# Retention and a routed MoE on one core: scores in 64x64 products without the empty corner, and each state update one step earlier

## The chip, the cores and the metric

The kernel runs on one core of a Trainium2 chip. The metric is the time of one execution on the device in microseconds (us); the kernel before has a median of 399.66 us over three runs. The engines are TensorE (PE; PEld are its weight loads), VectorE (DVE), ScalarE (ACT), GpSimd (POOL) and the transfer queues (SP issues most transfers). Each engine works through its own list in order.

## The reference

q, k and v have 4 batches, 8 heads, 768 positions and 64 dimensions per head. Each head carries a 64x64 state along the positions, and the result then goes, token by token, through one of 8 experts:

```python
for t in range(S):
    state = gamma * state + outer(k[:, :, t], v[:, :, t])      # gamma: one number per head
    y[:, :, t] = scale * q[:, :, t] @ state
x = y.transpose(0, 2, 1, 3).reshape(3072, 512)
expert = argmax(x @ w_gate, axis=1); p = softmax(x @ w_gate)
out[t] = p[t, expert] * (relu(x[t] @ w1[expert]) @ w2[expert])    # 512 -> 1024 -> 512
```

## The kernel before, in words

**Retention.** The 3072 positions are 24 chunks (`g`) of 128, six to a batch (`c = g % 6`). The heads are 4 pairs: `p` counts pairs, `r` is the half of the 128 partitions that a head of the pair sits on, and `p = 2 * m + o`. For each chunk:

- `load` (L217) brings q and k (turned, dimension on the partitions) and v and k (natural, position on the partitions), 1 MB. Chunks 0 to 4 come in two halves, later ones in one transfer. `scale` (L232) multiplies v by powers of gamma and gives `vs`, on GpSimd or, where the caller says so, on VectorE.
- `scores` (L242) makes k times q per head: 8 products of 64 rows by 128 columns, 128 columns moving, into two PSUM tiles `sp`, one for each `r`. Of each 128x128 result the part where a key lies behind its query is not wanted: VectorE multiplies each tile by the mask `causal` (L251) and gives `Sb`.
- `carry` (L268) multiplies the state after the chunk before (`ub`) by q into the PSUM tile `Y`; the first chunk of a batch has none. `output` (L280) adds `Sb` times `vs` to `Y`; VectorE multiplies `Y` by decay factors `G` into `xT` (L293), which frees `Y`.
- `update` (L255) adds k times `vs` to the state `U` in PSUM, and ScalarE copies it to `ub` (L266). The last chunk of a batch has none.
- `rows` (L297) turns `xT` back into token rows with transposes, and `logits` (L328) and `finish_logits` (L338) make the gate's logits for two chunks at a time.

**Gate.** The chunks are in groups (`GROUPS`, L44). For each group `choose` (seven VectorE instructions, L371 to L380, of which L378 writes `EA`) picks the expert of each token, `rank` (TensorE, L385) counts places, `slots`, `weights`, `advance` (VectorE) finish them, and GpSimd's `send_rows` (L314) scatters the rows of the tokens into one region per expert. Group 2 are chunks 12 to 15, group 3 chunks 16 and 17.

**Order.** The schedule is written by hand: the loop at L530 calls these steps in the order in which each engine gets them. In pass `g` TensorE has scores of chunk `g + 1`, carry of `g`, then on even passes the transposes, on some the logits or a ranking, then the update of `g` and the output of `g`. Ahead of the loop (L472 to L512) stand the first loads, ten matmuls on `ones` that keep TensorE busy (`warm`, L489), the masks, scores of chunk 0 and the matmul `decay`. After the loop the last groups are ranked, with pieces of the first expert's work (`early_pieces`, L780) set between as `fill`; these need the rows of 320 tokens, which `turn_early` (L439) turns and splits.

**Experts.** `moe_main` (L826) runs the experts 1 to 7, each in a dense stream of matmuls with two-part weights (`split`, L127). `put_rows` (L870) weighs and scatters the last rows of the last expert.

Of the kernel before, what the change touches and what calls it, by code (L numbers as in the profile page):

```python
# [20 lines left out]
P = 128  # L21
NP = H // 2
C = 128
CPB = S // C
# [17 lines left out]
WARM = 10  # L42
# [12 lines left out]
for _name, _w in (("cv", 6 * H), ("ratio", 6 * (H // 2)), ("iota", E), ("desc", E), ("tok4", NTOK), ("blk", NJ), ("ebase", E),  # L55
                  ("rev", E1), ("eid", E1), ("caps", E1), ("quad", 1), ("slot", 16), ("pos", 4), ("gates", NP * E),
                  ("ahead", P), ("causal", P), ("ident", P)):
    OFF[_name] = (_n, _n + _w)
    _n += _w
NCONST = _n  # L60
NFIRST = OFF["iota"][0]
NLOAD = OFF["ahead"][0]


def _constants():
    p = np.arange(P)
    c = np.zeros((P, NLOAD), np.float64)

    def put(name, v):
        a, b = OFF[name]  # L70
        c[:, a:b] = v

    gamma = 1.0 - 2.0 ** (-5.0 - np.arange(H, dtype=np.float64))
    put("iota", np.broadcast_to(p[None, 0:E].astype(np.float64), (P, E)))
    pos = (np.arange(6)[None, :] * C + p[:, None] + 1).astype(np.float64)
    put("cv", (gamma[None, None, :] ** (-pos[:, :, None])).reshape(P, 6 * H))
# [18 lines left out]
def retention_moe(ctx, tc, qkv, w1, w2, cst, gdec, out):  # L95
# [8 lines left out]
    causal = k_("causal")  # L104
# [93 lines left out]
    with ExitStack() as actx:  # L198
# [5 lines left out]
        ps_s = apool("ps_s", 2, space=PS)  # L204
# [19 lines left out]
        def turned(g, i):  # L224
            return qs[g][:, i].rearrange("a (p t) -> a p t", p=NP)
# [15 lines left out]

        def scores(g):  # L242
            Sb = wk.tile([P, 2, NP, C], F32, name="Sb")
            q, kt = turned(g, 0), turned(g, 1)
            sps = [ps_s.tile([P, NP, C], F32, name="sp") for _ in range(2)]
            for p in range(NP):
                for r in range(2):
                    nc.tensor.matmul(out=sps[r][:, p, :], lhsT=kt[half[r], p, :], rhs=q[half[r], p, :],  # L248
                                     start=True, stop=True)
            for r in range(2):  # L250
                nc.vector.tensor_tensor(out=Sb[:, r], in0=sps[r],  # L251
                                        in1=causal.unsqueeze(1).broadcast_to([P, NP, C]), op=ALU.mult)
            Sbs[g] = Sb
# [14 lines left out]
        def carry(g):  # L268
            c = g % CPB
            Y = Ys[g] = ps_1.tile([P, 2, DM], F32, name="Y", tag="Y")  # L270
            if c > 0:
                q = turned(g, 0)
                for m in range(2):
                    for o in range(2):
                        p = 2 * m + o
                        for r in range(2):
                            nc.tensor.matmul(out=Y[half[o], r, m * C:(m + 1) * C], lhsT=ubs[(g - 1) % 3][half[r], p, :],
                                             rhs=q[half[r], p, :], start=(m == 0), stop=False, skip_group_check=True)
# [18 lines left out]
        def rows(g, ps=None, tag="mm"):  # L297
# [4 lines left out]
            tr = (ps or ps_m).tile([P, NP, P], F32, name="tr", tag=tag)  # L302
# [25 lines left out]
        def logits(t):  # L328
            pool_, tag = (ps_m, "mt") if t in slow else (ps_s, "sp") if 2 * t + 2 >= NCH - 2 else (ps_1, "misc")
            L = pool_.tile([P, TW], F32, name="L", tag=tag)  # L330
# [108 lines left out]
        def turn_early(i):  # L439
# [3 lines left out]
            if i == 0:  # L443
                first["xt"] = rawp.tile([P, KD, EARLY], F32, name="xt0", tag="raw")
                first["x"] = [wp.tile([P, KD, EARLY], F32R, name=n, tag="w", bufs=11) for n in ("xh0", "xl0")]
                early.extend(early_pieces(tc, wk, wp, ps_m, ps_s, ps_1, wparts, first["x"], first))
            xt0, x = first["xt"], first["x"]
            part = pieces[1:] if i else pieces[:1]
            for j, w, _ in part:
                turn_slices(nc, xt0, first["xg"], j, w)  # L450
            for j, w, _ in part:
                cut_high(nc, x[0], xt0, j, w)
            for j, w, eng in part:
# [39 lines left out]
        ahead = k_("ahead")  # L493
        nc.gpsimd.iota(ahead, pattern=[[1, P]], base=0, channel_multiplier=-1, allow_small_or_imprecise_dtypes=True)
        for mask, test in ((causal, ALU.is_ge), (ident, ALU.is_equal), (us, ALU.is_gt)):
            nc.vector.tensor_scalar(out=mask, in0=ahead, scalar1=0.0, scalar2=None, op0=test)
        nc.vector.memset(run, 0.0)
# [8 lines left out]
        scale(0, nc.vector)  # L506
# [22 lines left out]
        last = NCH - 1  # L529
        for g in range(NCH):  # L530
# [10 lines left out]
            if g in ranked:  # L541
# [16 lines left out]
            if g == FULL + 1:  # L558
                update(g)
# [12 lines left out]
            if c < CPB - 1 and g not in (1, FULL + 1):  # L572
# [21 lines left out]
            if g in chosen or g == last:  # L594
                i = chosen.get(g, 4)
                s = stages[i] = gating(i)
                s["choose"]()
                s["soft"]()
            if g == last:
                mark_early()  # L600
            if g in ranked:
# [3 lines left out]
                if g != FULL + 1:  # L605
                    s["slots"]()
                s["advance"]()
# [25 lines left out]
        rows(last, ps_s, "sp")  # L633
# [146 lines left out]
def early_pieces(tc, wk, wp, ps_m, ps_s, ps_1, wparts, x, first):  # L780
# [22 lines left out]
    def result(f, part):  # L803
        if not accs:
            accs.extend(ps_s.tile([P, DM], F32, name="acc", tag="sp") for _ in range(2))
# [20 lines left out]
def moe_main(ctx, tc, wparts, fetch, split, xhl1, Z0, ident, buf, xg, fetch_rows, expert_at, mask7, slot_marks, natural, overflow,  # L826
# [43 lines left out]
    def put_rows(e, py, j):  # L870
# [3 lines left out]

        parts = (slice(0, 2), slice(2, 4)) if e == E1 and j == len(widths[e]) - 1 else (slice(0, 4),)
        for i, k in enumerate(parts):
            args = dict(out=sliced(yo[:w, :])[:, k], in_=featured(py[:w, :])[:, k])
            if i:
                nc.scalar.activation(func=AF.Copy, scale=meta[:w, j, 1:2], **args)
            else:  # L880
                nc.vector.tensor_scalar(in0=args["in_"], out=args["out"], scalar1=meta[:w, j, 1:2], scalar2=None,
                                        op0=ALU.mult)
# [290 lines left out]
```

## Time and profile before

| | |
|---|---|
| median of 3 runs | 399.66 us (399.08 to 399.91) |
| the profiled execution | 400.06 us |
| its span, first to last instruction | 398.3 us |
| TensorE busy | 390.3 us (98%), 3236 matmuls and 3236 weight loads |
| VectorE, ScalarE, GpSimd busy | 240.3, 142.4, 185.2 us |
| moved by transfers | 81.53 MB, mean 205 GB/s |

The profile is of one execution, so sums are made against its own time and then set against the median. A busy time is that in which at least one instruction of the engine is under way; matmuls overlap, so their starts say more than their busy time. An idle time stands with the engine that waited and with what released it; "issue" means that the profile shows no releaser.

### The profile page before, as it was taken

To read this page: it belongs to the slowest core of one execution; us is meant where nothing else is said; L and a number is where in the kernel's file an instruction comes from. 1 tells how busy PE (TensorE), PEld (TensorE's weight loads), DVE (VectorE), ACT (ScalarE), POOL (GpSimd) and SP (SyncE) were. 2 spreads that over 40 slices of the span, in tenths; PEclk is the share of its full clock that TensorE was granted. 3 is DMA by queue.
4 is the path that set the end of the run, shared out by engine and by line. 5 is a ranking of instruction groups with operands and counts; after the bars stand their busy time and mean duration, and the time that the engine had idled before them with its cause. 6 is when DMAs were issued, how large, how long until landed. Compare 5 with 4: busy or idle time off the path is not lost. (4 is left out here: it accounts for less than half of the span.)

```text
span 398.3 us, 8240 instructions
## 1 busy us (share of the span) xinstructions
PE 390.3 (98%) x3236; PEld 356.5 (89%) x3236; DVE 240.3 (60%) x468; ACT 142.4 (36%) x249; POOL 185.2 (46%) x176
## 2 busy tenths in 40 slices
PE   8999999999999999999999999999999999999994
PEld 4888878787899889999999999999999999999972
DVE  3555757685744578573866477477737657665310
ACT  2224435224411455531542344054334416423100
POOL 1647959655260517200584077028406813740741
PEclk9999999999999999999999999999999999999998
DMA  8999999975058839547452755465564647430111
GB/s 273 422 419 420 418 416 420 324 297 149 2 216 174 327 117 305 214 167 162 166 182 92 190 183 213 84 209 165 177 152 157 234 83 232 146 133 0 54 47 48
DMA packets 42316, 81.53 MB, mean 205 GB/s; under 512 B 4444, under 2 KB 18144, under 8 KB 39844
## 3 DMA queue, kind: packets, MB, share of 16 engines
q1 hardware_dynamic: 36768, 67.46, 51.2%
q0 software_dynamic: 5360, 13.49, 9.1%
q8 instruction: 26, 0.43, 0.4%
q14 instruction: 14, 0.11, 0.1%
q10 hardware_dynamic: 148, 0.04, 0.1%
HBM read 65.90 MB, written 15.68 MB: 205 GB/s over the span
## 5 line engine op out<-in xcount | busy, mean ns | idle before, releaser
L738 POOL DMA_INDIRECT out<-Z,sidx x90 | 104.9, 1165 | 138.8 <-DVE Z L894 113.5
L133 DVE TENSOR_TENSOR wlo<-raw,whi 128x1024 fp32r<-128x1024 f32 x54 | 65.5, 1215 | 14.1 <-ACT whi L132 13.8
L132 ACT CAST whi<-raw 128x1024 fp32r<-128x1024 f32 (+1 forms) x72 | 67.3, 950 | 7.3 <-DMA raw<-w 7.3
L1034 PE MATMUL py<-hl,whi 128*128 128x452 f32 (+5 forms) x192 | 67.0, 349 | 0.0
L1034 PE MATMUL py<-hh,wlo 128*128 128x452 f32 (+5 forms) x192 | 66.8, 348 | 0.0
L1034 PE MATMUL py<-hh,whi 128*128 128x452 f32 (+5 forms) x192 | 66.8, 348 | 0.0
L1014 ACT ACTIVATE hh<-ph 128x452 fp32r<-128x452 f32 (+6 forms) x56 | 28.3, 507 | 81.5 <-PE ph L1009 81.5
L1009 PE MATMUL ph<-xh,wlo 128*128 128x452 f32 (+6 forms) x224 | 50.1, 345 | 0.0
L1009 PE MATMUL ph<-xh,whi 128*128 128x452 f32 (+6 forms) x224 | 50.1, 345 | 0.0
L1009 PE MATMUL ph<-xl,whi 128*128 128x452 f32 (+6 forms) x224 | 50.0, 345 | 0.0
L1015 DVE SCALAR_TENSOR_TENSOR hl<-ph,hh 128x452 fp32r<-128x452 f32 (+6 forms) x56 | 32.0, 574 | 29.7 <-ACT hh L1014 29.2
L1009 PEld LDWEIGHTS ph<-xh,whi 128*128 128x128 f32 x224 | 40.8, 188 | 0.8
L1009 PEld LDWEIGHTS ph<-xh,wlo 128*128 128x128 f32 x224 | 40.8, 188 | 0.8
L1009 PEld LDWEIGHTS ph<-xl,whi 128*128 128x128 f32 x224 | 40.7, 188 | 0.7
L1034 PEld LDWEIGHTS py<-hh,wlo 128*128 128x128 f32 x192 | 36.0, 188 | 0.8
L1034 PEld LDWEIGHTS py<-hl,whi 128*128 128x128 f32 x192 | 36.0, 188 | 0.7
L1034 PEld LDWEIGHTS py<-hh,whi 128*128 128x128 f32 x192 | 36.0, 188 | 0.7
L251 DVE TENSOR_TENSOR Sb<-sp,cs 128x512 f32<-128x512 f32 x48 | 30.8, 684 | 7.4 <-PE sp L248 7.4
L760 ACT CAST xh<-buf 128x512 fp32r<-128x512 f32 (+7 forms) x26 | 14.3, 556 | 56.5 <-DVE buf L753 56.5
L133 POOL TENSOR_TENSOR wlo<-raw,whi 128x512 fp32r<-128x512 f32 (+1 forms) x18 | 24.9, 1403 | 12.7 <-ACT whi L132 10.5
L738 POOL DMA_INDIRECT x_sorted<-xrow,KEY x24 | 24.2, 1010 | 13.1 <-issue 6.5
L889 DVE STREAM_TRANSPOSE Z<-py 128x416 f32<-128x416 f32 (+3 forms) x24 | 15.0, 626 | 24.4 <-PE py L1034 24.4
(163 smaller groups left out, 535.3 us busy)
## 6 DMA issues: line engine op xcount, KB each, us to landing
raw<-w SPq DMA_DIRECT2D x32, 1024.0 KB, 5.6
qkv_w<-qkv SPq DMA_DIRECT2D x12, 1024.0 KB, 18.3
qkv_t<-qkv SPq DMA_DIRECT2D x7, 1024.0 KB, 17.8
qkv_t<-qkv SPq DMA_DIRECT2D x8, 512.0 KB, 6.8
buf<-x_sorted SPq DMA_DIRECT2D x12, 211.2 KB, 4.8
x_sorted<-cs SPq DMA_DIRECT2D x6, 260.0 KB, 5.6
buf<-x_sorted SPq DMA_DIRECT2D x8, 195.0 KB, 4.7
out<-Z,sidx POOLq DMA_INDIRECT x90
```

The costliest lines, as they stand in the source:

```text
L132: nc.scalar.copy(out=hi[:, h], in_=raw[:, h])
L133: engine.tensor_tensor(out=lo[:, h], in0=raw[:, h], in1=hi[:, h].bitcast(F32), op=ALU.subtract)
L251: nc.vector.tensor_tensor(out=Sb[:, r], in0=sps[r], in1=causal.unsqueeze(1).broadcast_to([P, NP, C]), op=ALU.mult)
L738: sc = tc.nc.gpsimd.indirect_dma_start(out=dst, out_offset=bass.IndirectOffsetOnAxis(ap=index, axis=0), in_=rows, in_offset=None, bounds_c ...
L760: nc.scalar.copy(out=xh[:, :, c0:c0 + w], in_=xt[:, :, t0:t0 + w])
L889: nc.vector.transpose(out=Zs[e][:, 0:nb, k, :], in_=py[:, 0:32 * nb].rearrange("p (j c) -> p j c", c=32))
L1009: nc.tensor.matmul(out=ph[:, :cap], lhsT=wparts[e, f // 4][a][:, kd, fo:fo + P], rhs=x[:, kd, :cap], start=(n == 0), stop=(n == 3 * KD - 1))
L1014: nc.scalar.activation(out=hh[:, :cap], in_=ph[:, :cap], func=AF.Relu)
L1015: nc.vector.scalar_tensor_tensor(out=hl[:, :cap], in0=ph[:, :cap], scalar=0.0, in1=hh[:, :cap].bitcast(F32), op0=ALU.max, op1=ALU.subtract)
L1034: nc.tensor.matmul(out=py[:, :cap], lhsT=a[:, f % 4, k * P:(k + 1) * P], rhs=x[:, :cap], **se)
```

## The change

- Scores: each of the 8 products becomes two. The first half of the keys (64) meets all 128 queries, the second half only the last 64; the empty corner is not computed. Each product is 64 rows by 64 columns. Heads with `o = 1` have the two halves of their keys exchanged (in natural k and v, in the powers `cv`, and in a second mask `swapped`), so four products in a row sit on the four quadrants of the array. The two PSUM tiles are now fixed (`sps`), and their corners are cleared once.
- The update of chunk `g + 1` stands behind the output of `g`, one step earlier than before; those of chunks 0 and 2 stay ahead of their outputs, that of chunk 1 goes behind its carry.
- The first loads: q and k are stored pair by pair, so that a quarter of a chunk holds both for two pairs of heads. Chunk 0 comes in four transfers, chunk 1 in three, and ScalarE's queue issues the constants ahead of `gdec`. The warming matmuls are 6, not 10, and scale of chunk 0 goes to GpSimd.
- Three moved steps: the choice of group 2 goes from the end of pass 16 to pass 17, behind the mask of scores 18 (its weights behind its slots); `turn_early` is no longer split around the output of chunk 22 but stands wholly behind it; the last rows of the last expert are weighed by one ScalarE instruction, where a VectorE and a ScalarE instruction took half each.

```diff
-WARM = 10
+WARM = 6
-        def turned(g, i):
-            return qs[g][:, i].rearrange("a (p t) -> a p t", p=NP)
+        def turned(g, i, r, p):
+            at = i * 2 * C + p % 2 * C
+            return qs[g][half[r], p // 2, at:at + C]
...
+        sps = [ps_s.tile([P, 2, 2 * C], F32, name=f"sp{r}") for r in range(2)]
         def scores(g):
-            for p in range(NP):
-                for r in range(2):
-                    nc.tensor.matmul(out=sps[r][:, p, :], lhsT=kt[half[r], p, :], rhs=q[half[r], p, :],
-                                     start=True, stop=True)
+            for m in range(2):
+                for t0 in (0, HC):
+                    for o in range(2):
+                        for r in range(2):
+                            p, side = 2 * m + o, half[o if t0 == 0 else 1 - o]
+                            nc.tensor.matmul(out=sps[r][side, m, o * C + t0:(o + 1) * C],
+                                             lhsT=turned(g, 1, r, p)[:, t0:t0 + HC], rhs=turned(g, 0, r, p)[:, t0:C],
+                                             start=True, stop=True, skip_group_check=True)
...
-        load(0, halves[0])
+        load(0, quarters[0])
+        nc.scalar.dma_start(out=cs[:, 0:NFIRST], in_=cst[:, 0:NFIRST])
         nc.scalar.dma_start(out=gs, in_=gdec)
-        nc.scalar.dma_start(out=cs[:, 0:NFIRST], in_=cst[:, 0:NFIRST])
-        load(0, halves[1])
-        for part in halves:
+        for part in quarters[1:]:
+            load(0, part)
+        for part in (halves[0], *quarters[2:]):
             load(1, part)
...
+        for r in range(2):
+            nc.vector.tensor_scalar(out=ahead[half[r]], in0=ahead[half[r]], scalar1=float((HC, -HC)[r]), scalar2=None,
+                                    op0=ALU.is_ge)
+            corner = sps[r].rearrange("a m (o c) -> a m o c", o=2)
+            for o in range(2):
+                nc.vector.memset(corner[half[1 - o], :, o, 0:HC], 0.0)
...
-        scale(0, nc.vector)
+        scale(0)
...
+            if g == FULL - 1:
+                choose_group(2)
+            elif g in ranked:
                 stages[ranked[g]]["weights"]()
...
-            if g == 1:
-                update(g)
             if g < last:
                 carry(g)
             if g == 1:
+                update(g)
                 scores(g + 1)
...
-            if g == FULL + 1:
-                update(g)
...
-            if c < CPB - 1 and g not in (1, FULL + 1):
+            if g in (0, 2):
                 update(g)
...
-            if g == last - 1:
-                turn_early(0)
             output(g)
+            if g > 1 and (g + 1) % CPB < CPB - 1 and g < last:
+                update(g + 1)
             if g == last - 1:
-                turn_early(1)
+                turn_early()
...
-        parts = (slice(0, 2), slice(2, 4)) if e == E1 and j == len(widths[e]) - 1 else (slice(0, 4),)
+        args = dict(out=sliced(yo[:w, :]), in_=featured(py[:w, :]))
+        if e == E1 and j == len(widths[e]) - 1:
+            nc.scalar.activation(func=AF.Copy, scale=meta[:w, j, 1:2], **args)
```

## Rows read from the trace of the kernel before

**Rows 1.** Windows: busy us (x instructions) of PE, PEld, DVE, ACT and POOL in three stretches, with the granted clock, the transfers' share and GB/s.

```profile
12.00:75.00 63.00, 63.00 (x1084) 50.81 (x1082) 39.06 (x84) 24.95 (x58) 46.36 (x47) 1.00 1.02 414
75.00:103.00 28.00, 27.20 (x456) 21.49 (x453) 21.36 (x60) 9.85 (x25) 13.96 (x17) 1.00 0.62 207
103.00:398.00 295.00, 289.38 (x1594) 277.98 (x1592) 175.18 (x311) 104.78 (x161) 122.36 (x105) 0.99 0.51 156
```

**Rows 2.** Waits of TensorE from 10 to 105 us, all that the view lists: who waited for whom, us in total, times, longest.

```profile
PE Y L287 <- issue: 0.6, 1, 0.6
PE Y L277 <- ACT xh L760: 0.2, 1, 0.2
```

**Rows 3.** Timeline of one pass (`g = 14`): start, length from the first start to the last end, engine, line, what, count, and in brackets the idle time before.

```profile
61.86 0.97 PEld L248 LDWEIGHTS sp<-qkv_t 64*128 64x128 f32 x16 [0.17 <-issue]
61.86 1.16 PE L248 MATMUL sp<-qkv_t 64*128 64x128 f32 x16
...
62.95 0.42 PEld L277 LDWEIGHTS Y<-qkv_w,ub 64*64 64x64 f32 x16
62.95 0.67 PE L277 MATMUL Y<-qkv_w,ub 64*64 64x128 f32 x16
...
63.55 0.85 PEld L304 LDWEIGHTS tr<-cs,xT 128*128 128x128 f32 x8 [0.17 <-issue]
...
63.91 1.28 DVE L251 TENSOR_TENSOR Sb<-sp,cs 128x512 f32<-128x512 f32 x2
...
64.37 0.10 PEld L387 LDWEIGHTS <-us 128*128 128x128 bf16 x1
...
64.73 0.55 PEld L263 LDWEIGHTS U<-vs,qkv_w 128*64 128x64 f32 x16
...
65.19 0.86 PEld L287 LDWEIGHTS Y<-Sb,vs 128*64 128x64 f32 x16
...
66.22 0.30 PEld L248 LDWEIGHTS sp<-qkv_t 64*128 64x128 f32 x4 [0.17 <-issue]
```

**Rows 4.** Timeline of the start, the same columns.

```profile
0.77 4.39 SPq L222 DMA_DIRECT2D qkv_t<-qkv  x8
...
1.08 4.35 PE L489 MATMUL warm<-ones 128*128 128x512 bf16 x10 [1.08 <-DVE ones L155]
...
1.32 0.36 ACTq L477 DMA_DIRECT2D cs<-cst  x1
...
5.36 1.16 PE L248 MATMUL sp<-qkv_t 64*128 64x128 f32 x16
...
6.64 0.69 DVE L235 TENSOR_TENSOR vs<-qkv_t,cs 128x512 f32<-128x512 f32 x1 [4.94 <-DMA cs<-cst]
...
7.25 1.28 DVE L251 TENSOR_TENSOR Sb<-sp,cs 128x512 f32<-128x512 f32 x2
7.50 0.55 PEld L263 LDWEIGHTS U<-vs,qkv_t 128*64 128x64 f32 x16 [0.76 <-DVE vs L235]
...
9.39 1.16 PE L248 MATMUL sp<-qkv_t 64*128 64x128 f32 x16
```

**Rows 5.** Timeline around scores of chunk 5: GpSimd's scale of that chunk and the weight loads of its scores.

```profile
20.99 1.04 POOL L235 TENSOR_TENSOR vs<-qkv_w,cs 128x512 f32<-128x512 f32 x1 [0.40 <-DMA qkv_w<-qkv]
...
22.14 0.97 PEld L248 LDWEIGHTS sp<-qkv_w 64*128 64x128 f32 x16 [0.17 <-issue]
```

**Rows 6.** Timeline of pass 17: the choice of group 2 on VectorE, output 17 and the ranking on TensorE.

```profile
76.09 0.19 DVE L371 TENSOR_REDUCE mx<-lg 128x4 f32<-128x32 f32 x1
...
77.10 0.19 DVE L378 TENSOR_TENSOR EA<-lp,ed 128x32 bf16<-128x32 f32 x1
77.17 0.19 PEld L287 LDWEIGHTS Y<-Sb,vs 128*64 128x64 f32 x3 [0.17 <-issue]
...
78.18 0.79 PEld L287 LDWEIGHTS Y<-Sb,vs 128*64 128x64 f32 x13 [0.82 <-issue]
...
79.14 0.10 PEld L387 LDWEIGHTS <-us 128*128 128x128 bf16 x1 [0.17 <-issue]
```

**Rows 7.** Timeline of the end of the retention: the turning of the early rows, carry 23, the first expert's first matmuls and `xT` of chunk 23.

```profile
99.59 0.71 DVE L753 STREAM_TRANSPOSE xt<-xg 128x512 f32<-128x512 f32 x1 [1.61 <-DMA xg<-x_sorted]
...
101.00 0.45 PEld L277 LDWEIGHTS Y<-qkv_t,ub 64*64 64x64 f32 x16 [0.43 <-ACT xh L760]
...
103.06 0.83 PE L793 MATMUL ph<-xh,whi 128*128 128x320 f32 x4
...
103.26 0.68 DVE L293 TENSOR_TENSOR xT<-Y,buf 128x512 f32<-128x512 f32 x1
```

**Rows 8.** Timeline of the end of the kernel: the last eviction in two halves, and the last scatter.

```profile
392.42 0.48 DVE L881 TENSOR_SCALAR yo<-py,meta 104x256 f32<-104x256 f32 x1 [4.81 <-PE py L1032]
392.94 0.47 ACT L879 ACTIVATE yo<-py,meta 104x256 f32<-104x256 f32 x1 [16.74 <-DVE yo L881]
393.72 1.01 POOL L738 DMA_INDIRECT out<-yo,sidx  x1 [4.86 <-ACTq L725]
```

**Rows 9.** The ScalarE group that evicts 512 columns of PSUM, up to 100 us: busy us, mean ns of one, idle time before.

```profile
L305 ACT COPY xrow<-tr 128x512 f32<-128x512 f32 x21 | 11.4, 590 | 24.0 <-PE tr L304 24.0
```

**Rows 10.** The page: GB/s in 40 equal slices of the span, and a transfer queue that fetches instructions: packets, MB, share.

```profile
GB/s 273 422 419 420 418 416 420 324 297 149 2 216 174 327 117 305 214 167 162 166 182 92 190 183 213 84 209 165 177 152 157 234 83 232 146 133 0 54 47 48
q8 instruction: 26, 0.43, 0.4%
```

More of the change, by code (lines that the diff above doesn't have):

```diff
@@ L23 @@
 C = 128
+HC = C // 2
 CPB = S // C
@@ L61 @@
 NFIRST = OFF["iota"][0]
-NLOAD = OFF["ahead"][0]
+NLOAD = OFF["causal"][0]
 def _constants():
@@ L277, in carry @@
                             nc.tensor.matmul(out=Y[half[o], r, m * C:(m + 1) * C], lhsT=ubs[(g - 1) % 3][half[r], p, :],
-                                             rhs=q[half[r], p, :], start=(m == 0), stop=False, skip_group_check=True)
+                                             rhs=turned(g, 0, r, p), start=(m == 0), stop=False, skip_group_check=True)
         def output(g):
@@ L295, in output, with rows @@
                                     in1=G[:, c].rearrange("a (r m) t -> a r m t", m=2))
-        def rows(g, ps=None, tag="mm"):
+        def rows(g, ps=None, tag="mm", tr=None):
             b, c = divmod(g, CPB)
@@ L301, in rows @@
                 xrows[b] = wk.tile([P, CPB, 4, SLICE], F32, name="xrow")
-            tr = (ps or ps_m).tile([P, NP, P], F32, name="tr", tag=tag)
+            if tr is None:
+                tr = (ps or ps_m).tile([P, NP, P], F32, name="tr", tag=tag)
             for p in range(NP):
@@ L328, in logits @@
         def logits(t):
-            pool_, tag = (ps_m, "mt") if t in slow else (ps_s, "sp") if 2 * t + 2 >= NCH - 2 else (ps_1, "misc")
-            L = pool_.tile([P, TW], F32, name="L", tag=tag)
+            if 2 * t + 2 >= NCH - 2:
+                L = sps[t - NCH // 2 + 2][:, 0]
+            else:
+                pool_, tag = (ps_m, "mt") if t in slow else (ps_1, "misc")
+                L = pool_.tile([P, TW], F32, name="L", tag=tag)
             for p in range(NP):
@@ L437, in fetch_early, with turn_early @@
             fetch_rows(xg0, 0, NJ0)
-        def turn_early(i):
+        def turn_early():
             pieces = [(a // 32, min(P, EARLY - a), eng)
                       for a, eng in zip(range(0, EARLY, P), (nc.gpsimd, nc.vector, nc.vector))]
[L443 to L449, printed above, removed]
+            xt0 = rawp.tile([P, KD, EARLY], F32, name="xt0", tag="raw")
+            first["x"] = x = [wp.tile([P, KD, EARLY], F32R, name=n, tag="w", bufs=11) for n in ("xh0", "xl0")]
+            early.extend(early_pieces(tc, wk, wp, ps_m, sps, ps_1, wparts, x, first))
+            for j, w, _ in pieces:
                 turn_slices(nc, xt0, first["xg"], j, w)
-            for j, w, _ in part:
+            for j, w, _ in pieces:
                 cut_high(nc, x[0], xt0, j, w)
-            for j, w, eng in part:
+            for j, w, eng in pieces:
                 cut_low(nc, eng, *x, xt0, j, w)
@@ L473, in retention_moe @@
         nc.vector.memset(wgs, 0.0)
-        load(0, halves[0])
+        quarters = [slice(i, i + 1) for i in range(4)]
+        load(0, quarters[0])
         gs = buf[0:2, 4 * NP * C:4 * NP * C + P + NP * C]
+        nc.scalar.dma_start(out=cs[:, 0:NFIRST], in_=cst[:, 0:NFIRST])
         nc.scalar.dma_start(out=gs, in_=gdec)
-        nc.scalar.dma_start(out=cs[:, 0:NFIRST], in_=cst[:, 0:NFIRST])
-        load(0, halves[1])
-        for part in halves:
+        for part in quarters[1:]:
+            load(0, part)
+        for part in (halves[0], *quarters[2:]):
             load(1, part)
@@ L492, in retention_moe @@
         keep_warm(WARM)
-        ahead = k_("ahead")
+        ahead = k_("swapped")
         nc.gpsimd.iota(ahead, pattern=[[1, P]], base=0, channel_multiplier=-1, allow_small_or_imprecise_dtypes=True)
-        for mask, test in ((causal, ALU.is_ge), (ident, ALU.is_equal), (us, ALU.is_gt)):
+        for mask, test in ((k_("causal"), ALU.is_ge), (ident, ALU.is_equal), (us, ALU.is_gt)):
             nc.vector.tensor_scalar(out=mask, in0=ahead, scalar1=0.0, scalar2=None, op0=test)
+        for r in range(2):
[4 more added lines that the diff above has]
+                nc.vector.memset(corner[half[1 - o], :, o, 0:HC], 0.0)
         nc.vector.memset(run, 0.0)
@@ L529, in retention_moe, with choose_group @@
         last = NCH - 1
+        def choose_group(i):
+            stages[i] = gating(i)
+            stages[i]["choose"]()
+            stages[i]["soft"]()
         for g in range(NCH):
@@ L593, in retention_moe @@
                 nc.scalar.copy(out=wgs[:, :, 0:E], in_=k_("gates").rearrange("p (k e) -> p k e", k=NP))
[L594 to L598, printed above, removed]
+            if g in chosen and g != FULL - 2:
+                choose_group(chosen[g])
+            if g == last:
+                choose_group(4)
             if g == last:
@@ L606, in retention_moe @@
                     s["slots"]()
+                if g == FULL - 1:
+                    s["weights"]()
                 s["advance"]()
@@ L632, in retention_moe @@
             send_rows(g)
-        rows(last, ps_s, "sp")
+        rows(last, tr=sps[0].rearrange("a m (o c) -> a (m o) c", o=2))
         fill(FILL[1])
@@ L777, in prep_slices, with early_pieces @@
     cut_slices(nc, engine, xh, xl, xt, j0, w, t0)
-def early_pieces(tc, wk, wp, ps_m, ps_s, ps_1, wparts, x, first):
+def early_pieces(tc, wk, wp, ps_m, sps, ps_1, wparts, x, first):
     nc = tc.nc
@@ L804, in result @@
         if not accs:
-            accs.extend(ps_s.tile([P, DM], F32, name="acc", tag="sp") for _ in range(2))
+            accs.extend(sps[1 - i].rearrange("p m c -> p (m c)") for i in range(2))
             both = ps_1.tile([P, 2, DM], F32, name="acc2", tag="Y")
@@ L873, in put_rows @@
         yo = yp.tile([P, DM], F32, name="yo")
-        parts = (slice(0, 2), slice(2, 4)) if e == E1 and j == len(widths[e]) - 1 else (slice(0, 4),)
[L876 to L882, printed above, removed]
+        args = dict(out=sliced(yo[:w, :]), in_=featured(py[:w, :]))
+        if e == E1 and j == len(widths[e]) - 1:
+            nc.scalar.activation(func=AF.Copy, scale=meta[:w, j, 1:2], **args)
+        else:
+            nc.vector.tensor_scalar(in0=args["in_"], out=args["out"], scalar1=meta[:w, j, 1:2], scalar2=None, op0=ALU.mult)
         scatter_rows(tc, out, index[:w, j:j + 1], yo[:w, :], "rows")
```

27 lines of the change are left out of this document (14 added, 13 removed).

## The prediction

> **What bounds the kernel now.** I read the windows first, then the waits, then the timeline of single chunks. The windows [rows 1] cut the span at the first settled chunk, at the end of the heavy loading and at the end of the retention. What to see there: TensorE is busy nearly all the time in all three, while VectorE is busy 39.06 of 63.00 us and then 21.36 of 28.00 us, and GpSimd 46.36 of 63.00 us. Up to 75 us the transfers are full too (share 1.02). A busy share of matmuls that overlap proves little, so the second view is TensorE's waits from 10 to 105 us [rows 2]: 0.6 us behind no releaser and 0.2 us behind a cast. TensorE therefore runs through its list without waiting, and a chunk lasts as long as its list. What shortens the list shortens the kernel, as long as nobody else becomes late.
>
> The timeline of one chunk [rows 3] prices the list by first starts: scores at 61.86, carry at 62.95, transposes at 63.55, ranking at 64.37, update at 64.73, output at 65.19, the next scores at 66.22. Scores cost 1.09 us, carry 0.60, eight transposes 0.82, the update 0.46, the output 1.03.
>
> **The price of a wave.** Eight products are sixteen matmuls, two each. The transposes use the whole array, one after another: 0.82/8 = 0.10 us for 128 columns. Scores use two halves of the rows: eight waves of two. Carry uses four quadrants: four waves of four, and costs 0.60. If a wave of 128 columns takes 0.11 us, scores are 8 x 0.11 = 0.88 plus 0.21, and carry 4 x 0.11 = 0.44 plus 0.16. The update has eight waves of two with 64 columns: 0.46/8 = 0.057 us each. The rest of 0.16 to 0.21 us belongs to the change of tile shape: weight loads stand idle 0.17 us ahead of scores and of transposes, whose shapes differ from their predecessors', and not at all ahead of the output, which has the update's shape, or of the ranking, which has that of the transposes [rows 3].
>
> **New scores.** Sixteen matmuls of 128 columns on four quadrants are four waves, 0.44 us; sixteen of 64 columns are four waves of 0.057, 0.23 us. Sum 0.67. They have carry's shape and carry follows at once, so one change of shape goes: 0.67 + 0.44 + 0.16 = 1.27 us where 1.09 + 0.60 = 1.69 stand now. That is **0.42 us a chunk**. No row shows 64 columns on four quadrants. The densest mean start of matmuls in rows is one per 0.44/16 = 0.0275 us (carry); if nothing starts denser, 32 matmuls take 0.88 us, and only the change of shape is saved, **0.21 us**. I take 0.42, since carry and update both keep their tiles streaming without a gap, and keep 0.21 as the bound.
>
> The Trainium skill (TensorEngine Tiling (Array Packing), Instruction Overhead) speaks against this part: a matmul has some 60 cycles of its own, and one should not take the factor from a dimension that is already small. If these cycles counted once for the whole array, an estimate from that page is 25 ns for each of 32 matmuls, 0.80 us, and 0.29 us saved. Counted in each tile, they would hide behind 64 columns. The carry row, at 27.5 ns, decides neither.
>
> **The start.** Scores of chunk 0 start at 5.36 when a 512 KB half has landed, VectorE's `vs` at 6.64 when the constants have, the update at 7.50, scores of chunk 1 at 9.39 [rows 4]. The first quarter is half as large, the constants are issued before `gdec` (now at 1.32), and VectorE can mask at once, since `scale(0)` goes to GpSimd (1.04 us there [rows 5], 0.69 on VectorE). I take 0.6 us earlier for scores of chunk 1; the ends are 0, if the constants land as late as now, and 0.9, if all follows a first transfer of 256 KB less at the 273 GB/s of the first slice [rows 10]. The added masks and four clearings on VectorE fall into its 4.94 us of waiting and cost nothing; without that cover six small instructions at 0.2 us, as VectorE's others [rows 6], would be 1.2 us. With 0.42 us for each of scores 1 to 4, and one update (the third's, 0.46) that now comes ahead of scores 5, TensorE could reach scores 5 at 22.14 - 0.6 - 1.7 + 0.46 = 20.3. But their chunk is one transfer, and GpSimd waits for it until 20.99 [rows 5]. The transfers are full there, their bytes stay, so I take 20.99: **1.15 us** gained, bounds 0.3 and 1.8.
>
> TensorE's clock: the ten warming matmuls take 4.35 us, 512 columns at the spacing of the lower level (1.2 GHz), and scores run at the upper (2.4 GHz) right after [rows 4]. Six end near 3.6 us, and TensorE then idles until the quarter lands. If the lower level lasts on to about 9 us, scores, `decay`, update and output of chunk 0 take twice their time, 1 to 2 us more; 0.7 of that hides behind the landing of chunk 5.
>
> **The settled chunks.** Scores 5 to 23 belong to 19 passes: 19 x 0.42 = **8.0 us** (with the bound 4.0). Sixteen updates fall into them now, fifteen after, since one has gone ahead: **0.46**. An update behind the output costs no more than one ahead of it, the shape is the same; its copy on ScalarE has a whole pass until carry needs it. It also gives VectorE 0.46 us more before carry needs `xT`.
>
> **The moved choices.** `choose_group(2)` now follows the mask of scores 18 on VectorE. Counted from the first of these scores: their end is at 0.67 + 0.28 (last start to end) = 1.0, the two masks take 1.28 [rows 3], and the choice up to EA takes 1.20 (76.09 to 77.10 + 0.19 [rows 6]); with the hand-overs EA is there at 3.6. TensorE gets to the ranking with 1.27 + 1.03 + 0.46 = 2.8 us, so it waits 0.8. Behind it VectorE is late with `scale`, `xT` and five slot instructions (0.69 + 0.69 + 5 x 0.2), so the masks of scores 19 and choice 3 slip, and I take 0.5 us more for the ranking of group 3. **Loss 1.3 us**, bounds 0 and 2.
>
> **The early expert's rows.** VectorE waits 1.61 us for them ahead of `xT`, and carry 23 stands 0.43 us [rows 7]. After, `xT` goes first: 0.43 gained. But three turnings and casts come later, and the first expert's matmuls (103.06) and the last `xT` (103.26), with the last choice behind it, by up to 0.8 us, of which I take 0.5; carry waits some 0.2 for `xT` (0.69 long, after an output that ends one transposition earlier). **Net loss 0.3**, bounds +0.4 and -0.8. From 103 us on the list is unchanged and moves as a whole; the weights' transfers have room there (share 0.51 [rows 1]).
>
> **The end.** VectorE's half (0.48) and ScalarE's half (0.47) of the last eviction run one after the other, 392.42 to 393.41 [rows 8]. One ScalarE instruction of 512 columns costs 0.59 [rows 9], ending at 393.02. **Gain 0.35.**
>
> **Instructions.** 24 chunks get 32 more each, 768, on top of 6472. Weight loads of output 17 stand 0.82 us with no releaser [rows 6] in the midst of a group, which looks like instructions arriving late; the page counts 26 fetches [rows 10]. The chunk of [rows 3] has some 158 instructions in 4.36 us, and would have 190 in 3.94, a third more per us, while the transfers are full. I take **0.4 us** lost, with bounds of 0.8 gained (this stall gone) and a stall at every fetch (below).
>
> By the Trainium skill (Runtime: NRT & Kernel Launch, Instruction fetch mechanics) blocks of 256 instructions are fetched ahead and mostly hidden; by that rule the term is 0, the sum 8.4 and the time 391.3, inside the forecast's own range. The stall in this trace does not fit it well.
>
> **Sum**: 1.15 + 8.0 + 0.46 - 1.3 - 0.3 + 0.35 - 0.4 = 8.0 us. The profiled execution took 400.06 us (span 398.3), the median is 399.66: 0.4 apart, so I take the sum from the median: **391.7 us**.
>
> **Rivals.**
> A: no denser starts than carry's. 19 x 0.21 in place of 0.42 takes 4.0 us away: 395.7. For it: no row is denser than 27 ns. Against: within carry the engine is limited by columns, four waves of 0.11. The Trainium skill's rule above, taken for the whole array, would be a weaker case of A.
> B: VectorE or the transfers become the bound between 60 and 100 us. VectorE's 21.36 us would stand in about 25 of TensorE's, 85%, and in-order behind `scale`, which waits for late chunks. If one in three of the 19 passes loses its 0.42 and the choices cost 2.0 us: 8.0 - 2.6 - 0.7 = 4.7, 395.0. For it: transfers are full up to 75 us, and TensorE reaches each chunk up to 7 us sooner. Against: the waits show VectorE holding up nothing now.
> C: the lower clock lasts to 9 us: 1 us more behind the cover, 392.7.
> D, on the other side: each fetch of the retention stalls TensorE 0.82 us. Half of TensorE's matmuls lie there (1540 of 3236 from 12 to 103 us [rows 1]), so about half of the 26 fetches, with the added instructions 16: 13 us lost against 8.4, 404 us. It decides from ten stalls on (8.4/0.82). Against: one such stall now.
> E, no change: neither the waves nor the change of shape get shorter. Without the 8.0 the rest cancels: 399.7. Against: carry, in that very shape, takes half of what scores take.
>
> **Chances.** Forecast 0.55 (own range 389.5 to 393.8), A 0.17, B 0.14, C 0.08, D 0.04, E 0.02. With the unknown bounds (clearest: the stall gone, no wait at the choices, the rows on time: 8.0 + 1.2 + 1.3 + 0.7 = 11.2, 388.5) the range is 388.5 to 396.0. Within 0.2% (0.8 us) is what a measurement of this kernel can't tell from no change: faster 0.94, same 0.02, slower 0.04.
>
> **What would show it.** Scores to carry 0.7 us and carry to the next 0.6 (A: 0.9); no idle ahead of carry; scores 5 near 21.0; scores 23 near 87; carry 23 some 8.5 us sooner than 101.00; the ranking at 17 behind EA; one ScalarE row at the end. Wrong: long idle stretches of weight loads without releaser, or `xT` late in front of carry in many passes.

## The result, and the profile after

The changed kernel is slower: 402.53 us (six runs, 401.30 to 404.22) against 399.64 us for the kernel before on the same chip, a ratio of 1.007 (95% interval 1.0052 to 1.0088). The forecast was 391.7 us, range 388.5 to 396.0. The profiled execution took 401.30 us, 1.24 us more than that of before. All comparisons inside traces below are of profiled executions.

The steps themselves came out as described. This is the timeline of one pass after (start, length, engine, line, what, count):

```profile
60.47 0.90 PE L257 MATMUL sp<-qkv_w 64*64 64x128 f32 x32
61.19 0.62 PE L286 MATMUL Y<-qkv_w,ub 64*64 64x128 f32 x16
61.74 0.44 PE L357 MATMUL lp<-cs,LT 128*128 128x128 f32 x2
```

Scores cost 61.19 - 60.47 = 0.72 us (1.09 in [rows 3]), carry 0.55, and nothing stands idle between them. But TensorE, which hardly waited before [rows 2], now has this in the view of waits from 10 to 105 us (who for whom, us in total, times, longest; the four largest of six):

```profile
PE sp L257 <- issue: 3.5, 4, 1.5
PE L L345 <- issue: 1.1, 2, 0.6
PE pf L400 <- DVE sh L393: 0.7, 1, 0.7
PE L L345 <- ACT wgs L615: 0.6, 1, 0.6
```

The first two lines have no releaser. One of these stops, in the midst of the 32 matmuls of one chunk's scores:

```profile
38.67 0.78 PE L257 MATMUL sp<-qkv_w 64*64 64x128 f32 x23
40.95 0.38 PE L257 MATMUL sp<-qkv_w 64*64 64x128 f32 x9 [1.51 <-issue]
```

Counting TensorE's records (each weight load, each matmul and each record of its sequencer is one instruction) shows where such stops stand. All seven between 20 and 75 us come exactly 256 instructions, or a multiple, after one another, and none of the instructions behind them waits for a semaphore. The trace has the packets of the queue that fetches instructions too (16 KB each). Worked out from both:

```
after: block begins at   first runs at (gap ahead)   next packet of the fetch queue
  #450                   15.82  (0.15)               19.62
  #706                   22.04  (0.36)               26.06
  #962                   28.34  (0.78)               32.17
  #1218                  34.65  (0.06)               38.56
  #1474                  40.95  (1.78)               44.51
  #1730                  46.90  (1.00)               50.84
  #1986                  53.21  (0.48)               57.18
  #2242                  59.47  (0.04)               63.22
  #2498                  65.59  (1.50)               69.15
  #2754                  71.51  (0.82)               75.39
  #3010                  78.34  (0.00)               81.93
  #3266                  84.39  (0.01)               86.43
  #3522                  89.74  (0.00)               90.15
```

Up to 75 us a fetch starts 3.6 to 4.0 us after the block before it was entered, and where TensorE stands waiting, the block runs 2.3 to 2.4 us after its packet's start. So while the transfers are full, TensorE gets 256 instructions per 6.2 us, 41 per us, however short its list is. The kernel before has the same grid, but passes 256 instructions in 6.4 to 8.3 us and was stopped by it once: 0.85 us at its #2498, the 0.82 us of [rows 6], behind a fetch that started 6.6 us after its block was entered. Its other fetches up to then started 1.7 to 3.6 us after, sooner than here; why they did is not shown. From 84 us on the fetch starts 0.4 to 2 us after the block is entered, and nothing stops. The windows show the transfers' share (the figure ahead of the last):

```profile
12.00:75.00 63.00, 57.74 (x1320) 46.95 (x1314) 38.25 (x83) 23.70 (x56) 44.43 (x46) 1.00 1.01 412
75.00:103.00 28.00, 26.98 (x591) 21.79 (x583) 22.19 (x61) 9.70 (x26) 15.15 (x19) 1.00 0.69 226
103.00:398.00 295.00, 290.44 (x1595) 278.27 (x1594) 176.55 (x312) 106.11 (x164) 123.58 (x106) 1.00 0.51 156
```

TensorE is busy 57.74 of 63.00 us where it was busy 63.00 [rows 1]. The start lost time too; windows and timeline (in the windows the granted clock is the third figure from the end):

```profile
4.00:7.40 3.40, 2.33 (x37) 1.36 (x39) 1.29 (x2) 0.55 (x1) 1.04 (x1) 0.96 0.92 319
7.40:10.80 3.40, 3.40 (x56) 3.07 (x59) 0.62 (x1) 0.41 (x2) 1.15 (x2) 0.53 1.01 337
...
5.20 0.56 PE L257 MATMUL sp<-qkv_t 64*64 64x128 f32 x16 [0.47 <-DMA qkv_t<-qkv]
...
8.12 1.96 PE L296 MATMUL Y<-Sb,vs 128*64 128x128 f32 x16
...
19.68 0.64 PE L345 MATMUL L<-xT,wgs 128*32 128x256 f32 x8 [0.65 <-ACT wgs L615]
...
19.14 0.37 ACT L276 COPY ub<-U 128x256 f32<-128x256 f32 x1 [1.03 <-PE U L273]
19.41 0.22 ACT L615 COPY wgs<-cs 128x32 f32<-128x32 f32 x1
```

TensorE's clock, at its upper level from 4.0 us, is at the lower one from 7.4 to 10.8 us, after stretches in which it waited for quarters; the output of chunk 0 takes 1.96 us, not about 1.1. And logits 0 wait for the copy of the gate's weights (`wgs`) on ScalarE, which now stands behind the copy of update 3. The whole, by first starts:

```
                         before    after   difference
scores 5                  22.14    23.53     +1.39
scores 18                 75.48    78.17     +2.69
scores 23                 95.36    96.57     +1.21
carry 23                 101.02   101.18     +0.16
first expert's matmuls   103.06   103.71     +0.65
last matmul              391.99   393.53     +1.54
last scatter             393.72   394.95     +1.23
```

### The profile page after: what moved, and what is told of

Read it like the earlier page. It is cut to its first block, busy times and chain, and to the rows that moved or that the text cites. A ratio compares the mean times of both kernels' runs of the same rounds, so it can differ in the third digit from the quotient of the medians.

```text
span 399.5 us, 9005 instructions
## 1 busy us (share of the span) xinstructions
PE 384.8 (96%) x3616; PEld 353.2 (88%) x3616; DVE 241.7 (61%) x472; ACT 141.9 (36%) x249; POOL 186.7 (47%) x177
```

## The experiments

Some runs were on chips on which the kernel before takes 408 us, not 400; the ratio to before on the same chip is given, and kernels are compared with each other where they shared one or had the same time of before. Theory T: the supply of instructions under full transfers binds TensorE. The rivals are named in the expectations.

**Twice the instructions in the kernel before.** Each product of carry and output becomes two of 64 columns (`n` is 0 and 1, and `t` is `m * C + n * C // 2`):

```diff
-    rhs=q[half[r], p, :], start=(m == 0), ...
+    rhs=q[half[r], p, t - m * C:t - m * C + C // 2], start=(m == 0 and n == 0), ...
```

> The kernel before with each product of carry and output split into two of 64 moving columns: the same columns, 64 more TensorE instructions in a chunk with a carry, 32 in one without. Theory T (while the transfers are full, TensorE gets its instructions in blocks of 256, one per 6.2 us): from 25.6 to 78.2 us before passes 1792 instructions; 2500 take 2500/256 x 6.2 = 60.5 us in place of 52.6, so 6 to 8 us slower, with idle stretches of 0.3 to 2 us at instruction numbers 256 apart. Rival R (instructions are always there, the loss of the change lies elsewhere): a wave of 64 columns takes half of one of 128 (0.057 against 0.11 us), so 0 to 1.5 us slower and no such stretches.

Ratio 1.028 (1.0261 to 1.0296), 11.6 us slower by the medians. Blocks are entered at 22.01, 28.11, 34.48, 40.62, 46.54 and 52.89, 6.2 us apart on average, five of the six after gaps of 0.8 to 1.7 us, as here at #1218:

```profile
32.91 0.71 PE L248 MATMUL sp<-qkv_w 64*128 64x128 f32 x7
34.48 0.72 PE L248 MATMUL sp<-qkv_w 64*128 64x128 f32 x9 [0.86 <-issue]
```

R falls, and T holds in kind. These five stops make 5.9 us, and the loss is larger than the 6 to 8 us expected; a second kind of stop (last section) stands in this trace too, from 57 us on.

**The old scores in the changed kernel.**

```diff
-    out=sps[r][side, m, o * C + t0:(o + 1) * C], lhsT=turned(g, 1, r, p)[:, t0:t0 + HC], rhs=turned(g, 0, r, p)[:, t0:C]
+    out=sps[r][:, m, o * C:(o + 1) * C], lhsT=turned(g, 1, r, p), rhs=turned(g, 0, r, p)
```

> The changed kernel with the scores of before again (8 products of 128x128 per chunk, 32 instructions fewer, natural k and v not exchanged); all else as changed. Theory T: a chunk passes its instructions slower than they come, so the stalls at 256 go; scores cost 0.42 us a chunk more; the two cancel: 401.5 to 404 us. Rival R (the new scores save their 8 us, and the moved choices, the start and the end lose 10): about 410 us.

Ratio 1.005 (1.003 to 1.007) on a chip where before takes 407.7 us; the change itself, where before takes 408.0, stood at 1.0137 (1.0094 to 1.018). So on these chips the new scores don't save anything; by the two ratios, from two chips, they cost. In the trace with the old scores no stop without a releaser stands at a block's begin (the one gap there, 1.04 us at #2754, is a ranking that waits for VectorE).

**The new scores without the transfers.**

```diff
 def load(g, part=slice(0, 4)):
+    if g > 5:
+        qs[g] = qs[g - 6]
+        return
```

> The changed kernel without the loads of chunks 6 to 23 (it leaves them out and computes on the data of chunks 0 to 5 again; the expert stage then has other counts, so only the retention is read). Theory T: with transfers nearly idle after some 25 us, fetches start 0.4 to 2 us after a block is entered, the stalls at 256 go, and scores 5 to carry 23 take about 71 us where the change takes 77.7. Rival R1 (instructions at this density are too slow whatever the transfers do): the stalls stay, about 77 us.

The retention alone is read (its 477.6 us include another expert stage). The window from 22 to 96 us:

```profile
22.00:96.00 74.00, 72.81 (x1685) 60.50 (x1675) 53.77 (x132) 29.88 (x73) 53.37 (x57) 1.00 0.36 126
```

With a share of 0.36 TensorE has no stop at a block's begin; 256 instructions pass in 4.5 to 6.6 us. Scores 5 to carry 23 take 71.4 us (24.19 to 95.56); in the change they take 77.65, in the kernel before 78.88. This is the gain of the forecast, nearly in full, and it is there only if the transfers are not.

**Easing the supply.** Loads of chunks 5 to 23 in four transfers; or each load at the end of the pass that leaves its buffer, with four buffers in turn, in both kernels (two transfers of weights then go out in passes 1 and 3):

```diff
-    nc.sync.dma_start(out=qs[g][:, part], in_=qkv[g][:, part])
+    for i in range(4):
+        nc.sync.dma_start(out=qs[g][:, i:i + 1], in_=qkv[g][:, i:i + 1])
...
-    early = AHEAD <= g < FIRST or g in MID
+    early = False
...
+    if g < NCH - AHEAD: load(g + AHEAD)
```

> The changed kernel with the transfers of chunks 5 to 23 in four of 256 KB each, so 2 KB in a row for a partition in place of 8 KB; bytes and order unchanged. Theory T1 (the fetch of a block waits behind data packets that its transfer engine already holds, some 3.8 us of them, so it shrinks with their size): the start of a fetch comes 1 to 2 us after the block before is entered, the stalls at 256 go, 396 to 398 us. Theory T2 (it waits for bytes or for its turn in time, whatever the packets' size): 3.6 to 4.0 us as now, 402 to 403 us. More issues on SP (0.38 us each) cost nothing, SP has 4.1 us per chunk.

Ratio 1.012 (1.0056 to 1.0185), not told apart from the change's 1.0137. Up to 75 us, fetches start 2.2 to 4.9 us after a block is entered, most 3.0 to 4.2, although the packets are smaller (10676 from 22 to 80 us, 5037 after). T1 falls: their length is not what the fetch waits for.

> The changed kernel with the loads of chunk g + 4 issued when chunk g leaves its buffer (four buffers in turn), so that the transfers carry 1 MB per chunk of TensorE's time and are no longer full after some 16 us; the same bytes. Theory T (a block of 256 TensorE instructions takes 6.2 us to come while the transfers are full, and much less when they are not): fetches start 0.5 to 2 us after a block is entered, the stalls at 256 go, 4 to 7 us faster than the change as it is, so 1 to 3 us or more under before. Rival R1 (the supply does not hang on the transfers): the stalls stay, time as the change. Rival R2 (a chunk now lands too late): TensorE or GpSimd waits for loads, slower.

> The kernel before with the same paced loads. Theory T: it passes 34 to 36 TensorE instructions per us and is supplied 41, so only its one stall of 0.85 us can go: 0 to 1 us faster than before. If paced loads help for another reason (fuller banks, GpSimd's transfers in the way), it gains as much as the changed kernel does.

1.0203 (1.0182 to 1.0225) and 1.0178 (1.0131 to 1.0225). Pacing did not empty the transfers of the changed kernel (350 GB/s or more in six of the ten slices up to 100 us): its fetches start 0.6 to 5.1 us after a block is entered, up to 75 us, and stops at 256 remain in it. TensorE waits for loads, 3.3 us in the changed kernel and 5.4 in the other. R2 came true, and the test of T in it is inconclusive.

**The start.** All of the old start, or WARM = 10 and the `wgs` copy one step ahead:

```diff
-WARM = 6
+WARM = 10
...
+    if g == 2: nc.scalar.copy(out=wgs[:, :, 0:E], ...)
     if g > 1 and (g + 1) % CPB < CPB - 1 and g < last: update(g + 1)
```

> The changed kernel with the start of before: ten warming matmuls, chunk 0 and 1 in two transfers each, gdec issued ahead of the constants, scale of chunk 0 on VectorE. If the start costs what the traces compare (scores of chunk 1 at 10.00 against 9.39 us, TensorE's clock at half from 7.4 to 10.8), scores 1 stand at 9.4 or sooner and the rest follows by 0.6 to 1.5 us: 401 to 402 us. If only the supply of instructions counts up to 78 us, and that begins at the first fetch, it gains under 0.5 us.

> The changed kernel with ten warming matmuls in place of six, and with the copy of the gate's weights on ScalarE ahead of the copy of update 3, not behind it. TensorE's clock should stay at its upper level through chunk 0 (1.5 us) and logits 0 should not wait for ScalarE (0.87 us). By theory T TensorE then reaches its next block's end sooner and waits there: 0.5 to 1.2 us faster than the change. Without T: 2 to 2.5 us faster.

1.0102 (1.008 to 1.0124) and 1.0087 (1.0071 to 1.0102), beside 1.0137 for the change:

> The changed kernel as it is, so that the others stand beside it on one chip: 1.007 of the time of before, as found.

That is 1.4 and 2.0 us, with intervals that overlap, so the times don't show a gain; the 2.0 us of after_start, taken as they stand, would be the case without T (2 to 2.5). But the profiled executions of after_start and of the change there take 411.75 and 411.36 us, and the trace of the first shows what T says: scores 1 stand at 9.10 (10.47 in the change on that chip), logits 0 don't wait, and at #706 all of it is given back:

```profile
20.50 0.61 PE L286 MATMUL Y<-qkv_t,ub 64*64 64x128 f32 x14
22.24 0.43 PE L286 MATMUL Y<-qkv_t,ub 64*64 64x128 f32 x2 [1.12 <-issue]
```

The change passes #706 at 22.34 there.

**The moved steps undone** (choice of group 2 and the early rows' turning):

```diff
-    if g == FULL - 1: choose_group(2)
...
-    if g in chosen and g != FULL - 2: choose_group(chosen[g])
+    if g in chosen: choose_group(chosen[g])
...
+    if g == last - 1: turn_early(0)
     output(g)
```

> The changed kernel with the choice of group 2 back at the end of pass 16 and the early rows' turning split around output 22 again. The prediction priced these at 1.3 and 0.3 us lost; the trace after shows 0.91 and 0.54 us of waits ahead of the rankings and 1.4 us lost from carry 23 on. They lie at 80 us and later, where the supply no longer binds: 1.5 to 2.8 us faster than the change, 0.4 to 0.7% of it.

1.0095 (1.0062 to 1.0129), no better than the change (1.007, and 1.0087 below). The wait ahead of ranking 2 is gone, but carry 23 stands 1.9 us behind the early rows. A miss: what the choice gives back, these rows take.

**New scores in the last batch alone**, in the kernel before, then in the first batch too (`SWAP = (3,)` and `(0, 3)`; the halves of natural k and v are exchanged in these batches alone; the last rows are weighed as in the change):

```diff
+    if g // CPB in SWAP:
+        for m in range(2): ...
+    else:
+        for p in range(NP): ...
```

> The kernel before with its start, order and choices, the new scores in chunks 18 to 23 alone (the last batch, issued from 75 us on, when the transfers ebb), and the last rows weighed by one ScalarE instruction. Theory T: the supply holds there, 6 x 0.42 + 0.3 = 2.8 us faster than before (0.7%). Rival (VectorE is then late for each ranking and carry, and takes it back): 0 to 1 us faster.

> As hybrid_last, with the new scores in chunks 0 to 5 too, ahead of the stretch in which TensorE used to run at 34 to 36 instructions per us. Scores 1 to 4 gain 0.42 us each, until chunk 5 lands: 1.1 us more than hybrid_last, 3.5 to 4 us faster than before (0.9 to 1%). Theory T allows it if blocks are not entered sooner than 6.2 us after one another; otherwise a part of the 1.1 us turns into stalls at 256.

1.0041 (1.0026 to 1.0056) and 1.0096 (1.0075 to 1.0117), both a miss. In hybrid_last output 17 to output 22 take 20.1 us, not 21.8; but 0.85 us of the difference is the stop of before, which lies within output 17, so five new scores pay 0.8 us there, not five times 0.37. The one late fetch of before now stops TensorE 2.11 us, ahead of output 17, and at the end:

```profile
100.84 0.71 DVE L779 STREAM_TRANSPOSE xt<-xg 128x512 f32<-128x512 f32 x1 [2.61 <-DMA xg<-x_sorted]
101.48 0.65 DVE L312 TENSOR_TENSOR xT<-Y,buf 128x512 f32<-128x512 f32 x1
...
102.25 0.45 PEld L296 LDWEIGHTS Y<-qkv_t,ub 64*64 64x64 f32 x16 [1.34 <-ACT xh L786]
```

The first turning waited 1.61 us in [rows 7]. In hybrid_both the weight loads of carry 23 stand 2.82 us, and the first batch gains nothing: blocks are entered at 9.66, 15.04 and, after a stop of 1.49 us, 21.62. From the start addresses of the early rows to the first expert's matmuls it takes 13.8 us before, 12.6 after, 14.4 and 15.8 in these two. Theory U takes this chain for a second floor; a fixed length it is not.

> The kernel hybrid_last (new scores in chunks 18 to 23 alone) with the early rows' turning wholly behind output 22, as in the change. Theory U (the early rows' chain, from the start addresses to the first expert's matmuls 12.6 to 15.8 us in every trace, is a floor, and in hybrid_last carry 23 stands 1.4 us behind it): the wait ahead of carry 23 goes, the first expert's matmuls still start 12.6 us or more after the start addresses, at 102.6 in place of 104.3: 1.7 us faster than hybrid_last, 399.4 us where before takes 399.7. Rival (the 1.3 us that hybrid_last loses come from the longer stall at 78 us alone): no change from hybrid_last.

1.0035 (1.0021 to 1.0048). Half a hit: the first expert's matmuls came at 102.27 (104.31), as U says, the weight loads of carry 23 stand 0.35, and yet the time stayed. The profiled run lost 0.9 us at 138 us, where a subtraction on VectorE took 2.46 us, as in the rows below.

**A version without the supply limit:** the changed order, new scores in the last batch alone, the old start, `wgs` ahead (hybrid_order); then the choice of group 2 put back as well (hybrid_choice).

> The changed kernel with 128x128 scores in chunks 0 to 17 and the new ones in 18 to 23, the start of before, and the copy of the gate's weights on ScalarE ahead of that of update 3. By theory T no stalls at 256; from scores 18 on it goes as the change does (18.4 us to scores 23), and the early rows' chain, by theory U, lets the first expert begin at 101 us or later: 398.6 us, 0.3% under before. If the moved choices or the updates cost more than they bring, it is at 400 us or above.

> hybrid_order with the choice of group 2 back at the end of pass 16, so that the ranking of pass 17 finds it ready (0.91 us, and up to 0.5 us at the next). If what sets the end behind carry 23 is the chain of early rows, the first expert's matmuls start 0.9 to 1.4 us sooner than in hybrid_order (at 99.6 to 100.0) and the kernel gains that, at most: 398.5 to 399 us where before takes 399.75. If the weights of expert 1, which landed at 131.6 to 131.8 us in before and in hybrid_order alike, set the end, the gain is lost at 138 us and it stays at 399.5 to 400.

> The changed kernel as it is, beside the two: 1.007 of before where before takes some 399.7 us, 1.014 where it takes some 408.

1.0003 (0.9994 to 1.0012), 0.9996 (0.9987 to 1.0004), and 1.0087 (1.0072 to 1.0103) for the change. The first missed its 398.6 us, the second came out near the worse of its two cases. Neither has a stop at 256, and carry 23 comes 2.8 and 3.1 us sooner than in before; of that 0.34 and 0.45 us are left at the last matmul. In hybrid_order it goes here:

```profile
100.92 0.85 PE L824 MATMUL ph<-xh,whi 128*128 128x320 f32 x4 [0.38 <-ACT xh L791]
...
133.03 4.75 POOL L136 TENSOR_TENSOR wlo<-raw,whi 128x1024 fp32r<-128x1024 f32 x2 [1.99 <-ACT whi L135]
135.88 2.46 DVE L798 TENSOR_TENSOR xl<-buf,xh 128x512 fp32r<-128x512 f32 x1 [1.71 <-ACT xh L791]
...
138.99 0.73 PE L955 MATMUL py<-whi,hT 128*128 128x512 f32 x2 [0.65 <-DVE hT L949]
```

The first expert's matmuls come only 2.1 us sooner, by the early rows' chain, and the two rankings behind them 1.6 and 1.25. Then GpSimd splits the next expert's weights, at a time that hangs on their landing (133.03 us, in before 132.81); VectorE's subtraction, which in before meets only the end of this and takes 0.99, falls under it and takes 2.46; TensorE waits (last row), and 0.9 of the 1.25 us are gone. So no version here beats the kernel before by more than the 0.2% that can be told.

## Why the prediction was wrong

- **Settled chunks (8.0 + 0.46).** The mechanism was right, and so was the price of a pass: scores 0.72 us, not 0.67, and carry 0.55, not 0.60, together the 1.27 of the sum. Without the transfers scores 5 to 18 take 48.4 us against 53.3; 0.46 of that is the update gone ahead, so 0.35 a chunk was there to be had, not 0.42. Rivals A and E fall. With the transfers the change took 54.6: the six stops in this stretch make 6.4 us, which covers the difference to 48.4.
- **Instructions (-0.4): the step that failed.** The prediction read the stop of [rows 6] as late instructions and counted a third more of them per us, but priced them as single stalls of a known length and gave rival D, whose 404 us came nearest, 0.04. The seven stops up to 75 us measure 6.7 us, not 0.4. It was a rate: 41 per us on offer; 36 asked for before; 190 in 3.94 us, 48, asked for by the forecast. The doubt, though not the rate, could be read in the trace of before: the late block there follows its packet by 2.2 us, and the packets up to then start 1.7 to 3.6 us after the blocks are entered, so 256 instructions per 3.9 to 5.8 us, 44 to 66 per us, and the 48 asked for lies between. The stop itself was an odd fetch, 6.6 us late, and told little of the others. Up to 78 us a saving in columns, bought with instructions, could only become idle time.
- The Trainium skill's rule (Runtime: NRT & Kernel Launch, Instruction fetch mechanics), by which the next block comes while one runs and the cost is mostly hidden, agrees in the blocks of 256, and holds here from 84 us on; under full transfers the trace disagrees, with 0.4 to 1.8 us of stop at the begin of seven of the ten blocks from #706 to #3010, which stood under them.
- **Start (+1.15, measured -1.39).** Scores 0 did come at 4.17, but the second half waited until 5.20, and rival C came true in another form: the clock was up at 4.0 us and fell afterwards, to 0.53 from 7.4 to 10.8; with ten warming matmuls (after_start, after_oldstart) it stays at 1.00 up to 14 us. Not seen at all was ScalarE's order: an update moved ahead takes its copy with it, past the `wgs` copy that logits 0 need.
- **Choices (-1.3).** Waits of 0.91 and 0.54 us, 1.45 in all, as worked out. But undoing this together with the early rows did not make it faster.
- **Early rows (-0.3, bounds +0.4 and -0.8).** From carry 23 to the last matmul 1.38 us were lost. The gain at carry came (carry 23 at +0.16 after scores 23 at +1.21), the first expert's matmuls waited 0.5 for their rows, and `xT` of chunk 23, behind all turnings, came 1.8 us later (105.05, 103.26), which moved the last choice. The bound of 0.8 was too small. The larger error is in the words "moves as a whole": behind 101 us stand two chains that don't move with TensorE, the early rows and the landing of the next weights.
- **End (0.35).** Last matmul to last scatter 1.73 before, 1.42 after: 0.31.
- **Rival B** (VectorE or the transfers) did not happen in its form: VectorE held up nothing but the rankings. The transfers did bind, though not through the data.

## What to carry to other kernels

Before cutting work into more instructions, count what the engine passes per us and what it is supplied in that stage: blocks of 256, and the time from one block's entry to the next block's arrival, both readable in the trace (here 41 per us under full transfers). A short stop without a releaser, in the midst of a group, is the sign to look for this supply; but it is the intervals at all blocks, also at those where nothing stops, that tell the rate, and not the length of the one stop. And behind a stage that is made shorter, look for the chain with a latency of its own: the two here gave back 2.4 of 2.8 us.

## What the runs showed of the hardware

- With TensorE waiting for them, its instruction blocks come 6.2 us apart on average under full transfers, and with shorter data packets the fetches start no sooner. Why a fetch starts some 3.8 us late there stays open; a few came 6.1 to 6.7 us late without a visible reason (before at #2242, after_third at #2754, where it cost 1.92 us more, which is also part of the spread of the change's times).
- On two chips, on which before takes 408 us, kernels with many instructions show a second kind of stop: in passes 10 and 16 of the change, while GpSimd scatters rows, TensorE halts some 0.5 us after every 8 to 11 instructions, and the passes take 7.2 and 7.7 us in place of 3.5 and 4.3. TensorE's timeline in pass 10 of the change there (after_again):

```profile
50.59 0.35 PE L257 MATMUL sp<-qkv_w 64*64 64x64 f32 x4 [0.32 <-issue]
51.34 0.26 PE L257 MATMUL sp<-qkv_w 64*64 64x64 f32 x1 [0.40 <-issue]
...
52.06 0.44 PE L286 MATMUL Y<-qkv_w,ub 64*64 64x128 f32 x4 [0.25 <-issue]
52.78 0.46 PE L286 MATMUL Y<-qkv_w,ub 64*64 64x128 f32 x6 [0.28 <-issue]
```

The cause was not found.

- VectorE's subtraction of two SBUF operands took 2.46 us when it started under GpSimd's (4.75 us for two), 0.99 in before, where it started under the last 0.44 us of them, and 0.68 clear of them (before, at 139.00). In both cases under GpSimd it ended 0.55 us after GpSimd did. The Trainium skill (SBUF — State Buffer, SBUF: two separate sides) has the two share a pair of ports that one of them holds for a whole instruction, and these rows agree.
- Sixteen products of 64 rows by 64 columns on four quadrants, two matmuls each, start 32 matmuls and their 32 weight loads in 0.72 us, 22.5 ns a matmul. This is denser than the 27.5 ns of carry and than the 25 ns that the prediction worked out for an overhead counted once for the whole array. So neither of the two is a least distance between starts.
